# A transformer block with Hedgehog linear attention: the sums of exponentials read in another order, and two softmaxes of the first block moved

## The chip, the cores and the metric

The kernel runs on one core of a Trainium2 chip. The metric is device time in microseconds (us) of one execution, the median of several. The core has a matrix engine (TensorE, PE in the profile, its weight loads PEld), a vector engine (VectorE, DVE), an engine for pointwise functions (ScalarE, ACT), a programmable one (GpSimd, POOL) and SyncE (SP), which here issues nearly all DMAs. Matmuls write PSUM, which VectorE and ScalarE read; all else lies in SBUF, 128 partitions wide.

## The reference

There are S = 2048 tokens of width 576, 32 heads of width 18, and a hidden width of 4608. What it computes, cut to the core:

```python
mod = silu(c) @ w_mod                      # six rows: sa, ca, ga, sb, cb, gb
h   = layernorm(x) * (1 + ca) + sa
q, k, v = split(h @ wqkv)                  # 32 heads of 18
pq, pk  = q @ w_phi[h], k @ w_phi[h]       # per head, 18 -> 18
phi_q = concat(softmax(pq), softmax(-pq))  # 36 features a head
phi_k = concat(softmax(pk), softmax(-pk))
kv, z = phi_k^T v, sum over s of phi_k
o = (phi_q kv) / (phi_q z + 1e-6)
x = x + ga * (o @ wo)
h = layernorm(x) * (1 + cb) + sb
x = x + gb * (relu(h @ w1) @ w2)
```

Each softmax is over the 18 features of one head of one token, so every token needs 64 sums of 18 exponentials for its queries and as many for its keys.

## The kernel before, in words

**Tiles.** Tokens lie in 16 tiles of 128 partitions. Heads are packed three to a group, 11 groups (the last has two heads and a zero one). Within a group the 54 columns are ordered by feature slot f (18) and then by head h (3): column f*3 + h. Beside them lie the 54 columns of the negated half, so a group's exponentials are 108 columns, first half s = 0, second half s = 1. A key tile holds its 11 groups at a distance of 108 elements (`phik`), a query pair in `Eqs` at a distance of 128. Elements are bf16, two bytes.

**Softmax** (`softmax_parts`, lines 392 to 485). For a block of four key tiles or a pair of query tiles (U = 2): `low` and `high` find minimum and maximum of every head by a tree of VectorE instructions (L401 to L406) and subtract them into the two halves (L412, L415); each is also there in parts, `low_root`, `low_less(j)`, `high_root`, `high_less(j)`. `exps(j)` takes the exponentials of one tile on ScalarE (L443). Then come the sums over the 18 slots, in one of two ways. `sums_pe(j)` (L445 to L452) sums for two tiles on TensorE: 18 matmuls, one for each slot f, with the identity as weights, accumulate 132 columns (2 tiles x 11 groups x 2 halves x 3 heads) in PSUM. `sums(j)` (L454 to L459) sums one tile on VectorE in one reduction. `recip(j)` takes Ln and Exp with scale -1 on ScalarE (L465, L467), and `scale(j)` multiplies the exponentials on VectorE (L474 for keys, L479 for queries). `split` is true for keys, whose sums are stored tile by tile.

**Order.** Scheduling is by hand: every engine runs its instructions in the order in which the program issues them. Phase 1 (up to line 753) follows a written list of steps, `order`: the folded weights, the norm, the projections (L385, one helper for k, v, q and the output projection), the keys' softmax with its eight `sums_pe` (steps `SU`), the softmax of query pair 0 with one (`qSU`), `phi_k^T v` (L564), and the first attention output. Phase 2 runs `block(n)` for the eight pairs of tiles n = 0 to 7. Block n does the feed-forward of pair n: `ffn1` for three hidden groups at a time (nine groups q, matmuls at L789 and L782, Relu on ScalarE at L794 with further work issued behind it), and `ffn2_step` in thirds of 12 matmuls (L821, then two VectorE instructions at L825 and L826 and a store). Between these it does the attention of pair n + 1: `attention(j)` is `num` (L605), the quotient on VectorE (L615 to L619) and a transpose by DMA (L630); `late(j)` is the output projection, the residual (L654) and the statistics; `norm_out` normalises and transposes by DMA (L363); `mods` modulates (L356). And it does the softmax of pair n + 2, ending in `q_T(n + 2)`, two DMA transposes from SP (L592) into `ET`, which `num` of the next block loads as weights.

**Block 0** is an exception: it also has the softmax of pair 1 (`soft1`), which its own attention needs. Before the change both `soft1` and the third pair's `soft_` (pair 2) do `low` and `high` first; pair 1's sums go to TensorE behind the fifth Relu; pair 2's exponentials go behind the seventh and eighth Relu, its sums, reciprocal, scaling and transposes to the end of the block, around the modulation.

Of the kernel before, what the change touches and what calls it, by code (L numbers as in the profile page):

```python
# [12 lines left out]
ACT = mybir.ActivationFunctionType  # L13
# [7 lines left out]
U = 2  # L21
# [20 lines left out]
def kernel(  # L42
# [34 lines left out]
    def aux_tile(name, dt=FP32):  # L77
        t = aux.tile([P, 512], FP32, name=name, tag="aux")
        return t if dt == FP32 else t.bitcast(BF16)
# [312 lines left out]
    def softmax_parts(E, src, n, split):  # L392

        ng = n * NG

        def view(j, s):
            return E[:, j, :, s * GF:(s + 1) * GF].rearrange("p g (f h) -> p g f h", h=GH)

        def ext(op):
            a9 = work.tile([P, 4 * NG, 27], BF16, name="tree", tag="tree", bufs=1)[:, 0:ng]  # L400
            V.tensor_tensor(out=a9.rearrange("p (n g) c -> p n g c", g=NG), in0=src[:, :, :, 0:27],  # L401
                            in1=src[:, :, :, 27:54], op=op)
            for w in (12, 6, 3):
                V.tensor_tensor(out=a9[:, :, 0:w], in0=a9[:, :, 0:w], in1=a9[:, :, w:2 * w], op=op)  # L404
            r = work.tile([P, 4 * NG, GH], BF16, name="root", tag="root", bufs=4)[:, 0:ng]
            V.tensor_tensor(out=r, in0=a9[:, :, 0:3], in1=a9[:, :, 24:27], op=op)  # L406
            return r.rearrange("p (n g) h -> p n g h", g=NG)

        def less(j, mn, mx):
            f = src[:, j].rearrange("p g (f h) -> p g f h", h=GH)  # L410
            if mx is None:
                V.tensor_tensor(out=view(j, 1), in0=mn[:, j].unsqueeze(2).to_broadcast([P, NG, DH, GH]),  # L412
                                in1=f, op=ALU.subtract)
            else:
                V.tensor_tensor(out=view(j, 0), in0=f,  # L415
                                in1=mx[:, j].unsqueeze(2).to_broadcast([P, NG, DH, GH]), op=ALU.subtract)

        t = {}

        def low_root():  # L420
            t["mn"] = ext(ALU.min)

        def low_less(j):
            less(j, t["mn"], None)

        def high_root():
            t["mx"] = ext(ALU.max)

        def high_less(j):
            less(j, None, t["mx"])  # L430

        def low():
            low_root()
            for j in range(n):
                low_less(j)

        def high():
            high_root()
            for j in range(n):
                high_less(j)  # L440

        def exps(j):
            A_.activation(out=E[:, j], in_=E[:, j], func=ACT.Exp)  # L443

        def sums_pe(j):  # L445

            ps = aux_tile("ps_sum")
            t[j] = ps[:, 0:2 * 2 * NG * GH]
            e = (E[:, j:j + 2].rearrange("p n g (s c) -> p n (g s) c", s=2) if split else
                 E[:, j:j + 2].rearrange("p n g (s c) -> p (n g) s c", s=2))  # L450
            for f in range(DH):
                T_.matmul(t[j], lhsT=ident[:], rhs=e[:, :, :, f * GH:(f + 1) * GH], start=(f == 0), stop=(f == DH - 1))  # L452

        def sums(j):  # L454
            if j == 0:
                t["l"] = work.tile([P, 132], FP32, name="ln_s", tag="ln_s", bufs=2)
                t[0] = t["l"][:]
            V.tensor_reduce(out=t["l"][:, j * 66:(j + 1) * 66].rearrange("p (g s h) -> p g s h", s=2, h=GH), op=ALU.add,
                            axis=mybir.AxisListType.X, in_=E[:, j].rearrange("p g (s f h) -> p g s h f", s=2, h=GH))  # L459

        def recip(j):
            ln_s = t.get("l")
            if ln_s is None:
                ln_s = work.tile([P, 132], FP32, name="ln_s", tag="ln_s", bufs=2)
            A_.activation(out=ln_s[:], in_=t[j], func=ACT.Ln)  # L465
            t["r", j] = work.tile([P, 132], BF16, name="rsum", tag="rsum", bufs=3)
            A_.activation(out=t["r", j][:], in_=ln_s[:], func=ACT.Exp, scale=-1.0)  # L467

        def scale(j):
            r = t["r", j][:].rearrange("p (a s h) -> p a s h", s=2, h=GH)  # L470
            if split:
                for i in range(2):
                    e = E[:, j + i].rearrange("p g (s f h) -> p (g s) f h", s=2, h=GH)
                    V.tensor_tensor(out=e, in0=e, in1=t["r", j][:, i * 66:(i + 1) * 66].rearrange("p (a h) -> p a h", h=GH)  # L474
                                    .unsqueeze(2).to_broadcast([P, 22, DH, GH]), op=ALU.mult)
                return
            for s in range(2):
                e = E[:, j:j + 2, :, s * GF:(s + 1) * GF].rearrange("p n g (f h) -> p (n g) f h", h=GH)
                V.tensor_tensor(out=e, in0=e, in1=r[:, :, s, :].unsqueeze(2).to_broadcast([P, 2 * NG, DH, GH]), op=ALU.mult)  # L479

        class parts:
            pass
        for f in (low_root, low_less, high_root, high_less, low, high, exps, sums_pe, sums, recip, scale):
            setattr(parts, f.__name__, staticmethod(f))
        return parts
# [101 lines left out]
    def q_T(n):  # L587
        E = Es[n]
        ET = work.tile([P, NG, U, P], BF16, name="ET", tag="ET", bufs=2)
        ETs[n] = ET  # L590
        for j in range(U):
            nc.sync.dma_start_transpose(out=ET[:, :, j, :], in_=E[:, j].rearrange("p g c -> p (g c)"))  # L592
# [243 lines left out]
    def block(n):  # L836


        m = n + 1 if n + 1 < NQ else None
        if m is None:  # L840
            for qs in ((0, 1, 2), (3, 4, 5), (6, 7, 8)):
                ffn1(n, qs)
            y(n, 0)

            y(n, 1, ((0, 288), (288, 192), (480, 96)))
            return
        soft_ = q_soft(n + 2) if n + 2 < NQ else None
        xn, stats, rstd, norm = norm_stats(m * U, U)

        def do(name, *a):  # L850
            if soft_ is not None:
                getattr(soft_, name)(*a)

        def attention(j):
            num(m, j)
            o_T(m, j)

        def late(j):
            wo_res(m, j)
            stats(j)  # L860

        def norm_out():
            rstd()
            norm()
            norm_dma(xn, U, new_hT2(m), 0)

        def mods():
            for ci in range(KC):
                modulate(V, hT2[m][:, ci, :], hT2[m][:, ci, :], mod[2], ci)

        if n == 0:
            soft1 = q_soft(1)
            for x in (soft1, soft_):
                x.low()
                x.high()
            ffn1(n, (0, 1, 2), {1: lambda: soft1.exps(0), 2: lambda: soft1.exps(1)})
            ffn1(n, (3, 4, 5), {4: lambda: soft1.sums_pe(0)})
            soft1.recip(0)
            soft1.scale(0)
            q_T(1)  # L880
            ffn1(n, (6, 7, 8), {6: lambda: do("exps", 0), 7: lambda: do("exps", 1)})
            ffn2_step(n, 0, 0, 288, 0)
            attention(0)
            ffn2_step(n, 0, 0, 288, 1)
            attention(1)
            ffn2_step(n, 0, 0, 288, 2)
            ffn2_step(n, 0, 288, 288, 0)
            late(0)
            ffn2_step(n, 0, 288, 288, 1)
            late(1)  # L890
            norm_out()
            do("sums", 0)
            ffn2_step(n, 0, 288, 288, 2)
            do("sums", 1)
            mods()
            do("recip", 0)
            do("scale", 0)
            q_T(n + 2)
            y(n, 1)
            return  # L900
        do("low")
        do("high")
        ffn1(n, (0, 1, 2), {1: lambda: attention(0)})
        ffn1(n, (3, 4, 5), {(3, "pairs"): lambda: attention(1), 3: lambda: do("exps", 0), 4: lambda: do("exps", 1),
                            5: lambda: late(0)})
        do("sums", 0)
        ffn1(n, (6, 7, 8), {7: lambda: late(1)})
        norm_out()
        do("sums", 1)
        ffn2_step(n, 0, 0, 288, 0)  # L910
        ffn2_step(n, 0, 0, 288, 1)
        ffn2_step(n, 0, 0, 288, 2)
        do("recip", 0)
        do("scale", 0)
        if n + 2 < NQ:
            q_T(n + 2)
        ffn2_step(n, 0, 288, 288, 0)
        mods()
        ffn2_step(n, 0, 288, 288, 1)
        ffn2_step(n, 0, 288, 288, 2)  # L920
        y(n, 1)
# [31 lines left out]
```

## Time and profile before

| | before |
|---|---|
| median of 3 runs | 435.09 us (435.04 to 435.96) |
| the profiled execution's own time | 435.43 us |
| its span, first to last instruction | 433.7 us |
| TensorE busy | 425.7 us (98%), 4147 matmuls |
| VectorE, ScalarE busy | 248.5 us (57%), 177.5 us (41%) |
| sums on TensorE (L452) | 180 matmuls |
| sums on VectorE (L458) | 12 reductions |
| granted TensorE clock, mean | 0.992 |

The page of the profile has the busy time of each engine, the span in 40 slices with the granted TensorE clock in tenths, the chain of work that ended last (followed back from the end, at each step to what released it), and the costliest groups of instructions. Matmuls are pipelined: the duration of a single matmul's row is longer than the time by which it delays the next, so what a matmul costs is read from the distance of starts, or from a group's length in the chain divided by its count.

### The profile page before, as it was taken

Reading aid. Unit: us, or ns where it says so; the run is one execution under the profiler, and the core shown is the slowest. Engines: PE = TensorE matmul, PEld = TensorE weight load, DVE = VectorE, ACT = ScalarE, POOL = GpSimd, SP = SyncE. Lnnn points to the kernel's source line nnn. Section 1 sums busy time; section 2 is a strip of 40 time slices with the busy share of each in tenths; the row PEclk is TensorE's granted clock in tenths of the full one; section 3 lists DMA queues with packets and bytes.
Section 4 is the critical chain, followed back from the end, with each engine's and each line's share of the span. In section 5 each row is a group of like instructions: output and inputs, shape, how many; then the busy total and the mean of one; then the engine's idle time right before and its main releaser. Section 6 shows DMA issues by size and latency. Waiting matters only on the chain.

```text
span 433.7 us, 9654 instructions
## 1 busy us (share of the span) xinstructions
PE 425.7 (98%) x4147; PEld 349.7 (81%) x4147; DVE 248.5 (57%) x627; ACT 177.5 (41%) x293; POOL 16.8 (4%) x55
## 2 busy tenths in 40 slices
PE   8999999999999998999999999999999999999997
PEld 4877888888788777878888887888788888878886
DVE  5998999986673695556562746455464712421011
ACT  4875987775466015402620451063026104302510
POOL 8300000000000000000000000000000000000000
PEclk9889999999999999999999999999999999999999
DMA  8965322008996154050114106110502231010000
GB/s 267 377 193 91 32 21 42 2 5 151 400 388 177 33 70 89 0 112 15 32 30 82 30 17 77 49 32 17 98 15 30 47 81 32 2 44 15 2 2 27
DMA packets 67188, 34.93 MB, mean 81 GB/s; under 512 B 53833, under 2 KB 63946, under 8 KB 67018
## 3 DMA queue, kind: packets, MB, share of 16 engines
q1 hardware_dynamic: 66544, 34.30, 32.2%
q8 instruction: 32, 0.52, 0.5%
q10 hardware_dynamic: 602, 0.02, 0.1%
q14 instruction: 10, 0.08, 0.1%
HBM read 19.63 MB, written 2.36 MB: 51 GB/s over the span
## 4 chain that ended last, share of the span: by engine, by line
PE 90%; DMA 5%; DVE 3%; SPq 1%; ACT 1%; issue 0%; DVEq 0%
PE ps_y L821 30%; PE ps_h L789 29%; PE ps_q L385 5%; PE ps_sum L452 4%; PE ps_k L385 4%; PE ps_wo L385 4%; PE ps_h L782 4%; PE ps_v L385 4%; DMA wma<-in_w_mod_dram 2%; DMA ET<-room 1%; PE ps_kv L564 1%; DMA oT<-o_tm 1%; PE ps_num L605 1%; DVE bst L190 1%; PE ps_mod L275 1%; PE ps_row L342 1%
## 5 line engine op out<-in xcount | busy, mean ns | idle before, releaser
L794 ACT ACTIVATE H<-ps_h 128x1024 bf16<-128x1024 f32 x72 | 73.6, 1022 | 173.0 <-PE ps_h L782 124.5
L821 PE MATMUL ps_y<-w_sb,H 128*128 128x288 bf16 (+2 forms) x1188 | 143.2, 282 | 0.0
L821 PEld LDWEIGHTS <-H 128*128 128x128 bf16 x1188 | 113.7, 98 | 27.3
L789 PE MATMUL ps_h<-hT,w1a 128*128 128x256 bf16 x640 | 74.9, 273 | 0.0
L789 PEld LDWEIGHTS <-w1a 128*128 128x128 bf16 x640 | 60.9, 98 | 10.3 <-issue 3.4
L825 DVE TENSOR_TENSOR outt<-ps_y,row_gb 128x288 bf16<-128x288 f32 (+2 forms) x33 | 14.8, 447 | 83.3 <-PE ps_y L821 83.2
L789 PE MATMUL ps_h<-hT,w1b 128*128 128x256 bf16 x512 | 60.5, 273 | 0.0
L385 PEld LDWEIGHTS <-hT 128*128 128x128 bf16 x480 | 46.4, 98 | 12.6 <-issue 1.0
L789 PEld LDWEIGHTS <-w1b 128*128 128x128 bf16 x512 | 49.5, 98 | 7.6 <-issue 1.7
L654 DVE TENSOR_TENSOR x_sb<-x_sb,ps_wo 128x288 bf16<-128x288 bf16 x28 | 12.7, 454 | 40.8 <-PE ps_wo L385 40.8
L404 DVE TENSOR_TENSOR tree<-tree 128x132 bf16<-128x132 bf16 (+3 forms) x72 | 24.4, 339 | 2.5
L190 DVE BATCH_NORM_STATS2 bst<-x_sb 128x6 f32<-128x288 bf16 x64 | 25.7, 443 | 0.1
L385 PE MATMUL ps_v<-wv_sb,hT 128*128 128x288 bf16 x160 | 21.7, 286 | 0.9 <-DVE room L85 0.9
L385 PE MATMUL ps_wo<-wo_sb,oT 128*128 128x288 bf16 x160 | 22.1, 286 | 0.5 <-DMA oT<-o_tm 0.5
L385 PE MATMUL ps_k<-wfold,hT 128*128 128x270 bf16 (+1 forms) x160 | 22.3, 291 | 0.0
L385 PE MATMUL ps_q<-wfold,hT 128*128 128x270 bf16 (+1 forms) x160 | 20.9, 285 | 0.0
L199 DVE TENSOR_SCALAR xn<-x_sb,mv,rstd 128x576 bf16<-128x576 bf16 x32 | 13.0, 452 | 12.1 <-ACT rstd L195 12.0
L782 PE MATMUL ps_h<-hT,w1c 64*128 64x256 bf16 x288 | 19.9, 271 | 0.0
L452 PEld LDWEIGHTS <-ident 128*128 128x128 bf16 x180 | 18.2, 103 | 1.4
L443 ACT ACTIVATE phik<-phik 128x1188 bf16<-128x1188 bf16 x16 | 18.7, 1187 | 1.2 <-DVE phik L415 1.1
L443 ACT ACTIVATE room<-room 128x1188 bf16<-128x1188 bf16 x16 | 18.9, 1185 | 0.7 <-DVE room L415 0.7
L385 PEld LDWEIGHTS <-oT 128*128 128x128 bf16 x160 | 15.5, 98 | 4.4 <-DMA oT<-o_tm 0.8
(139 smaller groups left out, 378.4 us busy)
## 6 DMA issues: line engine op xcount, KB each, us to landing
w_sb<-in_B_w_dram SPq DMA_DIRECT2D x4, 1296.0 KB, 15.6
out_dram<-outt SPq DMA_DIRECT2D x15, 144.0 KB, 1.9
w1b<-in_B_w_dram SPq DMA_DIRECT2D x1, 2048.0 KB
w1a<-in_B_w_dram SPq DMA_DIRECT2D x1, 1536.0 KB, 11.3
wma<-in_w_mod_dram SPq DMA_DIRECT2D x1, 1152.0 KB, 7.8
room<-in_A_wqkv_dram SPq DMA_DIRECT2D x2, 576.0 KB, 8.5
x_sb<-in_A_x_dram SPq DMA_DIRECT2D x1, 1152.0 KB, 9.8
wmb<-in_w_mod_dram SPq DMA_DIRECT2D x1, 1152.0 KB, 12.7
```

Of the source, the lines that this page charges most:

```text
L190: V.bn_stats(out=st[:, half, :], in_=x_sb[:, t0 + j, half * 288:(half + 1) * 288])
L199: V.tensor_scalar(out=xn[:, j, 0:D], in0=x_sb[:, t0 + j, :], scalar1=mv[:, j, 0:1], scalar2=rs[:, j:j + 1], op0=ALU.subtract, op1=ALU.mult)
L385: T_.matmul(ps[:, 0:cn], lhsT=lhs[:, ci, :], rhs=w[:, ci, cs:cs + cn], start=(ci == 0), stop=(ci == KC - 1))
L404: V.tensor_tensor(out=a9[:, :, 0:w], in0=a9[:, :, 0:w], in1=a9[:, :, w:2 * w], op=op)
L443: A_.activation(out=E[:, j], in_=E[:, j], func=ACT.Exp)
L452: T_.matmul(t[j], lhsT=ident[:], rhs=e[:, :, :, f * GH:(f + 1) * GH], start=(f == 0), stop=(f == DH - 1))
L654: V.tensor_tensor(out=xs[:, cs:cs + cn], in0=xs[:, cs:cs + cn], in1=p[:, 0:cn], op=ALU.add)
L782: T_.matmul(ps[q][:, e, hh * w:hh * w + w], lhsT=w1c[r, 2 * q + hh, :], rhs=hT[r, 4, :], start=(first and hh == 0), stop=(not first and hh ...
L789: T_.matmul(ps[q][:, e, hh * w:hh * w + w], lhsT=w1_at(4 * q + 2 * hh + e, ci), rhs=hT[:, ci, :], start=(first and hh == 0 and ci == 0), s ...
L794: A_.activation(out=H1[:, 4 * q:4 * q + 4, :].rearrange("p (h e) n -> p e h n", e=2), in_=ps[q][:].rearrange("p e (h n) -> p e h n", h=2), ...
L821: T_.matmul(ps[:, 0, 0:cn], lhsT=H1[:, k, j * P:(j + 1) * P], rhs=w2_sb[:, k, c], start=(k == 0), stop=(k == NJ - 1))
L825: V.tensor_tensor(out=o[:, c], in0=ps[:, 0, 0:cn], in1=rows["gb"][:, c], op=ALU.mult)
```

## The change

Two things change. First, the order in which `sums_pe` reads the exponentials of one slot: before, group by group with the three heads of a group next to each other; after, the head is the outermost of the free dimensions and the groups and halves the innermost. The sums then lie in PSUM in that order, and `recip` reads them by a rearranged view, so that `ln_s` and all after it are as before. `sums` gives its view of `ln_s` the same form.

Second, in block 0: `soft1`'s sums move from TensorE to VectorE, two reductions ahead of the second `ffn1`, with its reciprocal behind the fifth Relu. `soft_` (pair 2) is spread over the block: its maximum tree before `soft1`'s scaling, its subtraction of the maximum behind `q_T(1)`, its sums and reciprocal before the first third of `ffn2`, and its scaling and `q_T(2)` behind the second `attention`, where before they stood at the end.

```diff
         def sums_pe(j):
 
-            ps = aux_tile("ps_sum")
-            t[j] = ps[:, 0:2 * 2 * NG * GH]
-            e = (E[:, j:j + 2].rearrange("p n g (s c) -> p n (g s) c", s=2) if split else
-                 E[:, j:j + 2].rearrange("p n g (s c) -> p (n g) s c", s=2))
+            ps = aux_tile("ps_sum")[:, 0:2 * 2 * NG * GH]
+            if split:
+                e = E[:, j:j + 2].rearrange("p n g (s f h) -> p f h n (g s)", s=2, h=GH)
+                t[j] = ps.rearrange("p (h a) -> p a h", h=GH)
+            else:
+                e = E[:, j:j + 2].rearrange("p n g (s f h) -> p f h s (n g)", s=2, h=GH)
+                t[j] = ps.rearrange("p (h s a) -> p a s h", h=GH, s=2)
             for f in range(DH):
-                T_.matmul(t[j], lhsT=ident[:], rhs=e[:, :, :, f * GH:(f + 1) * GH], start=(f == 0), stop=(f == DH - 1))
+                T_.matmul(ps, lhsT=ident[:], rhs=e[:, f], start=(f == 0), stop=(f == DH - 1))
...
-            A_.activation(out=ln_s[:], in_=t[j], func=ACT.Ln)
+            o = ln_s[:].rearrange("p (a h) -> p a h", h=GH) if split else ln_s[:].rearrange("p (a s h) -> p a s h", s=2, h=GH)
+            A_.activation(out=o, in_=t[j], func=ACT.Ln)
...
             soft1 = q_soft(1)
-            for x in (soft1, soft_):
-                x.low()
-                x.high()
+            soft1.low()
+            soft1.high()
+            soft_.low()
             ffn1(n, (0, 1, 2), {1: lambda: soft1.exps(0), 2: lambda: soft1.exps(1)})
-            ffn1(n, (3, 4, 5), {4: lambda: soft1.sums_pe(0)})
-            soft1.recip(0)
+            soft1.sums(0)
+            soft1.sums(1)
+            ffn1(n, (3, 4, 5), {4: lambda: soft1.recip(0)})
+            soft_.high_root()
             soft1.scale(0)
             q_T(1)
-            ffn1(n, (6, 7, 8), {6: lambda: do("exps", 0), 7: lambda: do("exps", 1)})
+            for j in range(U):
+                soft_.high_less(j)
+            ffn1(n, (6, 7, 8), {6: lambda: soft_.exps(0), 7: lambda: soft_.exps(1)})
+            soft_.sums(0)
+            soft_.sums(1)
+            soft_.recip(0)
             ffn2_step(n, 0, 0, 288, 0)
             attention(0)
             ffn2_step(n, 0, 0, 288, 1)
             attention(1)
+            soft_.scale(0)
+            q_T(n + 2)
             ffn2_step(n, 0, 0, 288, 2)
             ffn2_step(n, 0, 288, 288, 0)
             late(0)
             ffn2_step(n, 0, 288, 288, 1)
             late(1)
             norm_out()
-            do("sums", 0)
             ffn2_step(n, 0, 288, 288, 2)
-            do("sums", 1)
             mods()
-            do("recip", 0)
-            do("scale", 0)
-            q_T(n + 2)
             y(n, 1)
```

More of the change, by code (lines that the diff above doesn't have):

```diff
@@ L456, in sums @@
                 t["l"] = work.tile([P, 132], FP32, name="ln_s", tag="ln_s", bufs=2)
-                t[0] = t["l"][:]
+                t[0] = t["l"][:].rearrange("p (a s h) -> p a s h", s=2, h=GH)
             V.tensor_reduce(out=t["l"][:, j * 66:(j + 1) * 66].rearrange("p (g s h) -> p g s h", s=2, h=GH), op=ALU.add,
```

## The prediction

> **What bounds the kernel now.** I read the page first (busy time, granted clock, the chain), then the chain in order of time, then every view of line 452, where the sums of exponentials are made.
>
> ```profile
> PE 425.7 (98%) x4147; PEld 349.7 (81%) x4147; DVE 248.5 (57%) x627; ACT 177.5 (41%) x293; POOL 16.8 (4%) x55
> ...
> PEclk9889999999999999999999999999999999999999
> ...
> PE 90%; DMA 5%; DVE 3%; SPq 1%; ACT 1%; issue 0%; DVEq 0%
> ```
>
> TensorE bounds the kernel: 98% busy, and 90% of the chain. A nanosecond added to its queue is a nanosecond of kernel, unless it fills one of its few holes. The chain in order of time shows the sums among the projections (a start, a length, the group):
>
> ```profile
> 28.91 2.00 PE ps_k L385 x10
> ...
> 49.27 1.92 PE ps_sum L452 x18
> 51.19 1.23 PE ps_k L385 x10
> ...
> 65.37 3.86 PE ps_sum L452 x36
> ...
> 82.17 2.01 PE ps_sum L452 x18
> ...
> 115.15 0.45 PE psT_n L369 x8
> ...
> 127.63 2.01 PE ps_sum L452 x18
> ```
>
> From 44 to 117 us the chain is TensorE without a gap, and ten sums lie on it: eight of keys (18 matmuls in 1.92 us, 106.7 ns each), two of queries (2.01 us, 111.7 ns each). That is slow. A projection's ten matmuls of 288 columns on average take 1.23 us, 0.427 ns a column, so 132 columns should take 56 ns; eight transposes of 128 columns, each with its own weights, do take 0.45 us, 56 ns each. What differs is the moving operand: for one slot it reads 44 runs of three elements (6 bytes), 108 bytes apart. The view of line 452 says what such runs cost (duration min/median/max in ns):
>
> ```profile
> L452 PE MATMUL ps_sum<-phik,ident x144: 268/275/282, 49.1 to 97.0; 128*128 128x132 bf16 x144
> L452 PE MATMUL ps_sum<-room,ident x36: 237/279/326, 82.0 to 129.4; 128*128 128x132 bf16 x36
> ```
>
> Key matmuls are all alike, query matmuls spread over 89 ns, with the same 44 runs and the same weights. Stepping through the timeline of the group at 127.47, starts follow each other after 128, 95, 130, 149, 96, 128, 94, 77 ns, and then again 126, 96, 128, 144, 95, 130, 95, 76. The period is 8 slots, 48 bytes: it is the address that counts. Query groups lie 256 bytes apart and their halves 108, and a boundary every 16 bytes fits: in slots 0, 2, 3 and 5 half of the runs straddle one (66 pieces), in 1, 4, 6 and 7 none does (44 pieces). For keys all halves lie 108 bytes apart, so a quarter straddles in every slot: 55 pieces, always alike. The time goes by pieces: (95+96+94+77)/4 = 90 ns for 44 is 2.06 ns a piece, (128+130+149+128)/4 = 134 for 66 is 2.03, 106.7 for 55 is 1.94; the lowest slot gives 77/44 = 1.75, the highest 149/66 = 2.26.
>
> **The change, part by part.**
>
> *The order of reading.* The new operand runs over the 44 groups and halves inside and the three heads outside. Neighbouring reads are now 108 or 256 bytes apart: 132 pieces of one element, not 55 of two or three. No row shows one-element pieces alone. Bounds: 1.75 x 132 = 231 ns a matmul and 2.26 x 132 = 298; below these stands only the contiguous 56 ns (a rival). I take 245 ns, 1.85 a piece: under the keys' 1.94, since a piece of one element has least to hand over, and above the one best slot. Keys: 144 x (245 - 106.7) = +19.9 us. The query sum that stays on TensorE (pair 0): 18 x (245 - 111.7) = +2.4. Together +22.3, all on the chain; with the bounds +20.0 to +30.9. VectorE and ScalarE get slack by it, so nothing is late behind them. [...]
>
> *The Ln.* Its nine inputs (L465, 0.28 us each) are now read from PSUM in steps and written in the old order. Bounds: nothing, or twice as long, 2.5 us on ScalarE in all; a gain is not excluded but would be as idle. Each stands between a sum and a scaling with other TensorE work between; I take 0.
>
> *First block: pair 1's sums on VectorE.* TensorE loses the group at 127.63: -2.0 us. VectorE gains two reductions:
>
> ```profile
> L458 DVE TENSOR_REDUCE ln_s<-room x12: 1334/1382/1384, 151.6 to 340.3; 128x66 f32<-128x1188 bf16 x12
> ```
>
> The timeline has the room for them on VectorE, and the wait that the next part is about on TensorE (start, length, idle before in brackets):
>
> ```profile
> 133.00 1.88 DVE L479 TENSOR_TENSOR room<-room,rsum 128x1188 bf16<-128x1188 bf16 x2 [4.68 <-ACT rsum L467]
> ```
>
> ```profile
> 164.50 0.41 PE L605 MATMUL ps_num<-KVZ,ET 108*128 108x57 bf16 x8 [1.18 <-DMA ET<-room]
> ```
>
> Two by 1.3 us fill most of the 4.68 us that VectorE idles ahead of its scaling. On times of before: they start when the third pair's subtraction from the minimum ends (125.5; the exponentials are done at 125.7) and end at 128.2; Ln and Exp behind the fifth Relu (ends 128.7) are done at 129.3, so the sixth Relu, queued behind them, starts about when its matmuls end; the maximum tree ends at 129.9, scaling at 131.8. The two transposes are issued 3.1 us earlier, and TensorE needs them 2.0 earlier: not late. Without VectorE's hole these reductions would cost up to 2.6 us.
>
> *First block: pair 2's softmax moved.* Nothing is added: the two subtractions, two exponentials, two reductions, Ln, Exp, two scalings and two transposes are done earlier. The exponentials wait for subtractions that end at 132.3 and 132.8, as Relus 7 and 8 (131.5 and 133.7) finish, so Relu 8 behind the first is not held. The reductions fall into VectorE's 4.36 us of idling ahead of the first quotient (139.24 in before, 137.2 now), the second until 137.4: +0.2 us for that quotient and for the transposed outputs behind it, where TensorE already waits 0.49 us at 147.27. I count +0.2 (bounds 0 and +1). The scaling, 1.88 us, now stands ahead of an output's eviction and the first residual; VectorE idled 1.28 us there and again 1.32 before the second, so it is covered. On SP the two transposes pass the output store and the transposes of the normalised rows (issued from 151.76) and stand behind those of the attention output; SP has nothing between 144 and 151.7, and their issue takes 3.98. POOL's fills of o_tm are not passed. What goes is the wait of the row at 164.50: TensorE waits 1.18 us there for ET, issued at 159.01. Next in line is the modulated hT, done at 157.15 against TensorE's need at 158.9: 1.7 us of margin, so the whole -1.2 is had.
>
> **Sum.** 435.43 (the profiled execution: span 433.7 and 1.7 around it) + 22.3 - 2.0 - 1.2 + 0.2 = 454.7; it ran 0.3 above the median of 435.09, so 454.4 us. Bounds 231 and 298 give 452.1 and 463.0.
>
> **Rivals.**
>
> *The clock drops in the sums* (chance 0.30). Each stretch, us, then busy time of TensorE, weight loads, VectorE, ScalarE, POOL, and the granted clock:
>
> ```profile
> 26.00:29.41 3.41, 3.41 (x80) 3.00 (x78) 3.31 (x13) 2.38 (x8) 0.28 (x1) 1.00 0.78 224
> 29.42:32.83 3.41, 3.41 (x19) 2.15 (x17) 3.31 (x12) 2.86 (x8) 0.00 (x0) 0.50 0.09 20
> ```
>
> The first stretch was full of matmuls by count, but 60 of them have one column; streamed columns fill about a third of it. In the next 3.41 us the clock is 0.50, and ten ps_k at 28.91 take 2.00 us, not 1.23. The sums now stream 56/245 = 23% (before 53%, where the clock held), and a group of 18 lasts 4.4 us, longer than such a stretch. If waiting for operands counts as idle, most of the seven places with sums (five single, two double) bring a drop that costs the work behind it up to 1.7 us; at 1.0 each, +7: 461 us, between 458 and 470. Against: nobody has idled; the array is held, not empty. [...]
>
> *Not slower: the price hangs on the weights, not on the order* (0.07). Each sum matmul loads the identity anew (180 loads, 103 ns mean), near the 106.7 ns spacing; if the load sets it, the order changes nothing and only block 0 moves: 435.1 - 3.0 = 432.1. This decides if a one-element piece costs under 0.8 ns. Against: 56 ns transposes also load 128 columns each time, and the query slots' 77 to 149 ns. [...]
>
> *Faster: the price is per run* (0.06). Six runs of 22 would stand in place of 44 of three; at the contiguous 56 ns, 144 x 50.7 + 18 x 55.7 = 8.3 us less: 423.8. For it: short runs are slow now. Against: with runs unchanged, straddling alone moves the price from 95 to 130.
>
> **How the numbers follow.** The forecast has 0.57; with the clock's rival 0.87 for slower. Faster has the other two, 0.12, less 0.01 for the weights' rival with block 0's gain lost. About 0.2% is what a measurement here can tell from no change. The range runs from the low bound less what the pieces' price may still be under (448) to the clock's rival with most of its spread (468): of the 0.87 it leaves out some 0.05, so it holds 0.82.
>
> **What the profile will show.** Right: groups of ps_sum x18 of about 4.4 us in the chain, 162 and not 180 matmuls on that line, none after 117 us plus the shift; two more reductions on VectorE (14); no wait for ET at the first num of block 1; from there to the end the blocks unchanged. Clock rival: stretches at 0.5 behind the sums. Wrong: a group of 1.0 us (price per run) or still 1.9 (weights).

## The result, and the profile after

The changed kernel takes 464.11 us (460.28 to 466.24), before it took 435.09: 6.5% slower, ratio 1.0652 with a 95% interval of 1.0578 to 1.0726. That lies inside the range that was given (448 to 468), 9.7 us above the forecast of 454.4 and 3 above the first rival's 461: the forecast's price came true, and the rival's drops of the clock came on top of it. The profiled execution took 465.03 us, its span is 463.2. The spread of the changed kernel, 6 us, is new; before it was 0.9.

The same lines of the page of after: busy time, granted clock in 40 slices, the chain by engine and by line.

```profile
PE 455.5 (98%) x4129; PEld 356.3 (77%) x4129; DVE 252.6 (55%) x629; ACT 177.6 (38%) x293; POOL 16.8 (4%) x55
...
PEclk9799879797889999999999999999999999999999
...
PE 90%; DVE 5%; DMA 3%; ACT 1%; issue 0%; SPq 0%
PE ps_y L825 29%; PE ps_h L793 27%; PE ps_sum L455 9%; PE ps_q L385 5%; PE ps_wo L385 4%; PE ps_v L385 4%; PE ps_k L385 4%; PE ps_h L786 4%; DVE bst L190 2%; DMA wma<-in_w_mod_dram 2%; PE ps_kv L568 1%; DMA oT<-o_tm 1%; PE ps_num L609 1%; DVE xn L199 1%; DVE mv L191 1%; DVE room L85 0%
```

TensorE has 18 matmuls less and is busy 30 us longer, and the clock, full after the start before, now has dents in slices 5 to 12 (0.86 as the mean from 40 to 150 us). The chain in order of time has both (start, length, group):

```profile
49.20 1.23 PE ps_bias L329 x10
50.43 4.58 PE ps_sum L455 x18
55.01 2.40 PE ps_k L385 x10
57.41 2.40 PE ps_v L385 x10
...
75.51 9.13 PE ps_sum L455 x36
84.64 5.12 PE ps_k L385 x30
...
101.69 4.09 PE ps_sum L455 x18
105.77 2.35 PE ps_v L385 x10
```

A key group takes 4.58 us (254 ns a matmul; 106.7 before), the query group 4.09 (227 ns). And projections right behind take 2.40 us for ten, not 1.23. The account up to the first matmul of the first feed-forward (117.0 us before, 149.9 after, +32.9) closes:

| | us |
|---|---|
| the nine sums of phase 1: 4.58 + 4.55 + 9.13 + 4.57 + 4.09 + 4.57 + 9.13 = 40.6, before 17.4 | +23.2 |
| slowed groups behind them: three of ten by 1.17, ps_q 0.17, ps_k 1.44, ps_v 1.12, ps_q 1.08, ps_kv 1.14 | +8.5 |
| the start, up to ps_bias (49.20, before 48.04) | +1.2 |
| block 0 and the wait in block 1: 313.3 us from the first feed-forward matmul to the end, before 316.65 | -3.3 |

The sum is +29.6 us, the difference of the spans (463.2 - 433.7 = 29.5). The start isn't the change's: up to 49 us the two programs differ in nothing that runs, and the first experiment's profile, with the old order, has the same lateness (first feed-forward matmul at 118.5).

That the slowed groups are the clock's work is in the view by stretches of after, which are cut on the grid of 3.41 us on which the clock changed in this trace (length, TensorE busy and count, weight loads, VectorE, ScalarE, POOL, then the granted clock):

```profile
49.92:53.33 3.41, 3.41 (x18) 1.75 (x16) 3.17 (x8) 2.54 (x5) 0.90 (x2) 1.00 0.96 43
53.33:56.74 3.41, 3.41 (x16) 1.98 (x15) 3.20 (x8) 0.59 (x2) 0.00 (x0) 0.50 0.00 0
...
94.29:97.70 3.41, 3.41 (x21) 2.06 (x20) 1.95 (x5) 2.18 (x4) 0.00 (x0) 1.00 0.02 5
...
101.12:104.53 3.41, 3.41 (x19) 1.86 (x18) 1.34 (x4) 2.17 (x2) 0.00 (x0) 1.00 0.00 0
104.53:107.94 3.41, 3.41 (x16) 2.03 (x15) 0.00 (x0) 1.13 (x3) 0.00 (x0) 0.50 0.00 0
```

TensorE counts as busy without a gap in all of them. Adding up streamed columns at 0.427 ns each (a projection's 1.23 us for 2880; an estimate), the stretch from 49.92 has 30% and the one from 101.12 has 34%, and each is followed by one at half clock; the one from 94.29 has 55% and the one from 97.70 has 41%, and the clock held behind both.

### The profile page after: what moved, and what is told of

Same layout as the page of the kernel before. It is cut to its first block, busy times and chain, and to the rows that moved or that the text cites. A ratio compares the mean times of both kernels' runs of the same rounds, so it can differ in the third digit from the quotient of the medians.

```text
span 463.2 us, 9618 instructions
## 1 busy us (share of the span) xinstructions
PE 455.5 (98%) x4129; PEld 356.3 (77%) x4129; DVE 252.6 (55%) x629; ACT 177.6 (38%) x293; POOL 16.8 (4%) x55
## 3 DMA queue, kind: packets, MB, share of 16 engines
HBM read 19.63 MB, written 2.36 MB: 47 GB/s over the span
## 4 chain that ended last, share of the span: by engine, by line
PE 90%; DVE 5%; DMA 3%; ACT 1%; issue 0%; SPq 0%
PE ps_y L825 29%; PE ps_h L793 27%; PE ps_sum L455 9%; PE ps_q L385 5%; PE ps_wo L385 4%; PE ps_v L385 4%; PE ps_k L385 4%; PE ps_h L786 4%; DVE bst L190 2%; DMA wma<-in_w_mod_dram 2%; PE ps_kv L568 1%; DMA oT<-o_tm 1%; PE ps_num L609 1%; DVE xn L199 1%; DVE mv L191 1%; DVE room L85 0%
## 5 line engine op out<-in xcount | busy, mean ns | idle before, releaser
L793 PEld LDWEIGHTS <-w1a 128*128 128x128 bf16 x640 | 60.9, 98 | 10.3 <-issue 3.4
L385 PEld LDWEIGHTS <-hT 128*128 128x128 bf16 x480 | 49.7, 105 | 17.6 <-issue 1.0
L455 PE MATMUL ps_sum<-phik,ident 128*128 128x132 bf16 x144 | 37.5, 436 | 0.0
L455 PEld LDWEIGHTS <-ident 128*128 128x128 bf16 x162 | 19.6, 121 | 19.7
L478 DVE TENSOR_TENSOR phik<-phik,rsum 128x1188 bf16<-128x1188 bf16 x16 | 15.0, 979 | 25.7 <-ACT rsum L471 25.7
L190 DVE BATCH_NORM_STATS2 bst<-x_sb 128x6 f32<-128x288 bf16 x64 | 25.7, 444 | 0.1
L385 PE MATMUL ps_k<-wfold,hT 128*128 128x270 bf16 (+1 forms) x160 | 25.4, 318 | 0.3 <-ACT room L83 0.3
L385 PE MATMUL ps_v<-wv_sb,hT 128*128 128x288 bf16 x160 | 24.1, 306 | 0.7 <-DVE room L85 0.4
L385 PE MATMUL ps_q<-wfold,hT 128*128 128x270 bf16 (+1 forms) x160 | 22.2, 297 | 0.0
L461 DVE TENSOR_REDUCE ln_s<-room 128x66 f32<-128x1188 bf16 x14 | 19.0, 1366 | 1.9 <-ACT room L443 1.9
```

The lines of the kernel that those rows point to most:

```text
L190: V.bn_stats(out=st[:, half, :], in_=x_sb[:, t0 + j, half * 288:(half + 1) * 288])
L385: T_.matmul(ps[:, 0:cn], lhsT=lhs[:, ci, :], rhs=w[:, ci, cs:cs + cn], start=(ci == 0), stop=(ci == KC - 1))
L455: T_.matmul(ps, lhsT=ident[:], rhs=e[:, f], start=(f == 0), stop=(f == DH - 1))
L793: T_.matmul(ps[q][:, e, hh * w:hh * w + w], lhsT=w1_at(4 * q + 2 * hh + e, ci), rhs=hT[:, ci, :], start=(first and hh == 0 and ci == 0), s ...
```

## The experiments

**The old order back.** The changed kernel, with `sums_pe` and `recip` as before:

```diff
-                e = E[:, j:j + 2].rearrange("p n g (s f h) -> p f h n (g s)", s=2, h=GH)
...
+            e = (E[:, j:j + 2].rearrange("p n g (s c) -> p n (g s) c", s=2) if split else
...
-                T_.matmul(ps, lhsT=ident[:], rhs=e[:, f], start=(f == 0), stop=(f == DH - 1))
+                T_.matmul(t[j], lhsT=ident[:], rhs=e[:, :, :, f * GH:(f + 1) * GH], start=(f == 0), stop=(f == DH - 1))
```

> The changed kernel with the old order of reading in sums_pe and recip; block 0 stays as changed. Theory (each separate piece of 16 bytes that a sum matmul touches costs about 1.9 ns, and the slow sums then let the clock drop): key groups are back at 1.92 us and query groups at 2.01, no stretch at clock 0.5 after 40 us, and block 0's two moves are all that is left: 435.1 - 2.0 - 1.2 + 0.2 = 432.1 us. Rival (block 0's moves cost something that the slow phase 1 hides, on VectorE or in the transposes): 435 or more, with a new wait in block 0.

Measured: 432.53 us beside 435.87 for the kernel before on the same chip, ratio 0.9926 (0.9913 to 0.9939). It was expected at 432.1. So the whole loss hangs on the order of reading, and block 0's moves are a gain of 3.3 us. This kernel is faster than both.

**The new order alone.** The reverse: the kernel before with the new `sums_pe` and `recip`, block 0 untouched.

> The kernel before with the new order of reading alone; block 0 as before, so ten groups of sums on TensorE. Theory: groups as in the changed kernel (4.57 us of keys, 4.09 of queries), the drops of the clock in phase 1, and one more slow group in block 0, 2.1 us longer: 464.1 + 4.1 + 1.2 - 0.2 = 469.2 us, some 34 above before, with a spread of several us between executions. Rival (the order costs only its matmul time, 8 x 2.65 + 2 x 2.08 = 25.4 us, and the rest of the 29 us came from block 0): 460.5.

Measured: 468.09 us (466.86 to 470.71), ratio 1.0752 (1.072 to 1.0783), 32.2 us above before; 469.2 was expected by the theory and 460.5 by the rival that took the matmul time alone. Its profile has half-clock stretches from 75.7 to 82.5, 96.2 to 113.2, 120.0 to 130.3 and 161.0 to 164.4 us, other places than in the changed kernel, though the groups are the same. Its grid of 3.41 us lies otherwise: one stretch starts at 51.78 us, in the changed kernel one at 49.92.

**Eighteen patterns in one kernel.** In the kernel before, the eighteen matmuls of each key sum read 132 elements in eighteen different patterns, one per line:

```diff
-            for f in range(DH):
-                T_.matmul(t[j], lhsT=ident[:], rhs=e[:, :, :, f * GH:(f + 1) * GH], start=(f == 0), stop=(f == DH - 1))
+            mm(o, lhsT=ident[:], rhs=x[:, 0:132], start=True, stop=False)
+            mm(o, lhsT=ident[:], rhs=st(2), start=False, stop=False)
...
+            mm(o, lhsT=ident[:], rhs=run(3, 24, 0), start=False, stop=False)
+            mm(o, lhsT=ident[:], rhs=run(3, 24, 6), start=False, stop=False)
...
+            mm(o, lhsT=ident[:], rhs=e[:, :, :, 17 * GH:18 * GH], start=False, stop=True)
```

Here `st(k)` reads every k-th element, and `run(m, k, o)` runs of m elements at a distance of k, from offset o (elements of two bytes).

> The kernel before, but the eighteen matmuls of each key sum read 132 elements in eighteen patterns, one on a line each: contiguous; single elements 4, 6, 8, 12, 16 and 18 bytes apart; 44 runs of three 48 bytes apart, starting on a 16-byte boundary or straddling one; 66 runs of two 32 bytes apart, likewise; 33 runs of four 64 bytes apart, likewise; 22 runs of six 96 apart; runs of four 16 apart; single elements 36 bytes apart; the new order; the old order. The sums of the keys are therefore not the reference's: the true sums are left out. Theory of pieces (about 1.9 ns for each 16-byte piece, or 0.42 a column where that is more): contiguous 56 ns; 4 bytes apart 33 pieces, 63 ns; 8 apart 66 pieces, 127; 16 and more apart 132 pieces, 253; runs of three aligned 44 pieces, 84, and straddling 88 pieces, 169; runs of two 127 and 253; runs of four 63 and 127; runs of four 16 bytes apart 63. Rival (a price per jump, each step that is not to the next element): all patterns of single elements alike at about 253, runs of three 84 whether they straddle or not, runs of two 127, runs of four 63. Rival (the weights' load): all near 107.

The chain of this kernel, one matmul a row (start, length):

```profile
49.17 0.06 PE ps_sum L466
49.23 0.06 PE ps_sum L467
49.29 0.09 PE ps_sum L468
49.38 0.12 PE ps_sum L469
49.49 0.18 PE ps_sum L470
49.67 0.23 PE ps_sum L471
49.90 0.24 PE ps_sum L472
50.15 0.08 PE ps_sum L473
50.23 0.16 PE ps_sum L474
50.38 0.12 PE ps_sum L475
50.50 0.24 PE ps_sum L476
50.74 0.06 PE ps_sum L477
50.80 0.11 PE ps_sum L478
50.91 0.06 PE ps_sum L479
50.97 0.06 PE ps_sum L480
51.03 0.23 PE ps_sum L481
51.27 0.26 PE ps_sum L482
51.53 0.11 PE ps_sum L483
```

| line | pattern | 16-byte pieces | us | ns a piece |
|---|---|---|---|---|
| L466 | contiguous | 17 | 0.06 | columns set it |
| L467 | single elements 4 bytes apart | 33 | 0.06 | 1.8, or the columns |
| L469 | single, 8 apart | 66 | 0.12 | 1.8 |
| L470 | single, 12 apart | 99 | 0.18 | 1.8 |
| L471 | single, 16 apart | 132 | 0.23 | 1.7 |
| L473 | runs of three, aligned | 44 | 0.08 | 1.8 |
| L474 | runs of three, straddling | 88 | 0.16 | 1.8 |
| L475 | runs of two, aligned | 66 | 0.12 | 1.8 |
| L476 | runs of two, straddling | 132 | 0.24 | 1.8 |
| L477 | runs of four, aligned | 33 | 0.06 | 1.8, or the columns |
| L478 | runs of four, straddling | 66 | 0.11 | 1.7 |
| L482 | the new order | 132 | 0.26 | 2.0 |
| L483 | the old order | 55 | 0.11 | 2.0 |

The time goes with the pieces, at 1.7 to 2.0 ns each, as long as the columns don't take longer; the five patterns that the table leaves out fit as well. Why the two orders of the kernel pay 2.0 and the other patterns 1.7 to 1.8 isn't shown. That the pieces are of 16 bytes is in the single elements: 0.06, 0.12, 0.18 and 0.23 us at 4, 8, 12 and 16 bytes, and no more than 0.24 at 18 (L472). A price per jump is out: single elements cost 0.06 to 0.24 us with 132 jumps each, and 66 runs of two double their time by a shift of 14 bytes (L475, L476). The weights are out: all eighteen load the same identity and take 0.06 to 0.26 us. The patterns also say what the new order did: 132 elements out of 132 pieces, where the old order got them out of 55.

**Dense matmuls in between.** To tell whether the low share of streaming brings the drops, the changed kernel gets a matmul of 324 columns between each two matmuls of a sum (contiguous for keys, three runs of 108 for the query sum):

```diff
-            ps = aux_tile("ps_sum")[:, 0:2 * 2 * NG * GH]
+            full = aux_tile("ps_sum")
+            ps = full[:, 0:2 * 2 * NG * GH]
...
             for f in range(DH):
+                if f:
+                    T_.matmul(full[:, 132:456].rearrange("p (g c) -> p g c", g=3), lhsT=ident[:], rhs=E[:, j, 0:3], start=False, stop=False)
                 T_.matmul(ps, lhsT=ident[:], rhs=e[:, f], start=(f == 0), stop=(f == DH - 1))
```

> The changed kernel with a matmul of 324 contiguous columns between each two of a sum's matmuls, into columns of the same bank that nobody reads: 17 more in each of nine groups, 153 by 0.138 us = 21.1 us more work on TensorE, which raises the share of time in which columns stream within a group from 22% to about 48%. Theory (the drops come from sums that stream too little within a window of 3.41 us; in the changed kernel windows under 0.35 dropped and those from 0.40 did not): no stretch at clock 0.5 between 40 us and the end, which gives the 8.5 us of slowed projections back: 464.1 + 21.1 - 8.5 = 476.7 us, and a spread between executions of under 1 us as before the change. Rival (the drops come with time, or the slowed projections have another cause): 485 us, with the same stretches at 0.5.

Measured: 478.07 us (475.9 to 478.9). Of the chain, a sum's matmul and the projections right behind the first sum:

```profile
50.33 0.26 PE ps_sum L458
...
57.21 1.23 PE ps_k L385 x10
```

The view by stretches of this kernel, one in the middle of a double group and one over all of phase 1:

```profile
83.07:86.48 3.41, 3.41 (x19) 1.88 (x18) 1.63 (x4) 0.00 (x0) 0.00 (x0) 1.00 0.01 2
...
40.00:160.00 120.00, 120.00 (x949) 81.69 (x947) 66.99 (x137) 53.98 (x112) 1.21 (x4) 1.00 0.21 46
```

The clock is 1.00 throughout; in the changed kernel it is 0.86 between 40 and 150 us. The sums still take 0.25 us each, and the projections behind them are back at 1.23 us for ten. The time is 1.4 us from the theory's 476.7 and 7 from the rival's 485: 21.1 us of added work cost 14.0. That the share of streaming brings the drops is shown; the spread stayed at 3 us, against the theory's 1, and that is open.

**Block 0, one move at a time**, both with the old order of reading, as edits of the kernel before. First only pair 1's:

```diff
-            for x in (soft1, soft_):
-                x.low()
-                x.high()
+            soft1.low()
+            soft1.high()
+            soft_.low()
...
-            ffn1(n, (3, 4, 5), {4: lambda: soft1.sums_pe(0)})
-            soft1.recip(0)
+            soft1.sums(0)
+            soft1.sums(1)
+            ffn1(n, (3, 4, 5), {4: lambda: soft1.recip(0)})
+            soft_.high_root()
...
+            for j in range(U):
+                soft_.high_less(j)
```

> The old order of reading, and of block 0's changes only pair 1's (its sums on VectorE, and what was put around them); pair 2's sums, reciprocal, scaling and transposes stand at the end of the block as before. Theory: TensorE has one group of 2.0 us less and nothing else moves on the chain; the wait for ET at the first num of block 1 stays at about 1.2 us: 435.4 - 2.0 = 433.4 us, 0.9 above the kernel with both. Rival (VectorE's two reductions come late for the first transposes): 434.5 or more, with a wait for ET in block 0.

Then only pair 2's, with pair 1's sums on TensorE as before:

```diff
+            do("sums", 0)
+            do("sums", 1)
+            do("recip", 0)
             ffn2_step(n, 0, 0, 288, 0)
             attention(0)
             ffn2_step(n, 0, 0, 288, 1)
             attention(1)
+            do("scale", 0)
+            q_T(n + 2)
...
-            do("sums", 0)
             ffn2_step(n, 0, 288, 288, 2)
-            do("sums", 1)
             mods()
-            do("recip", 0)
-            do("scale", 0)
-            q_T(n + 2)
```

> The old order of reading, pair 1 as before the change (its sums on TensorE), and only pair 2's sums, reciprocal, scaling and transposes moved ahead, as in the change. Theory: the wait for ET at the first num of block 1 is gone, 1.2 us, less 0.2 for the first quotient: 435.4 - 1.0 = 434.4 us. Rival (the transposes moved ahead get in the way of the attention output's, so that the output projection waits longer): 435.4 or more, with a longer wait for oT than 0.5 us.

Measured, beside 435.47 for the kernel before: 432.81 (ratio 0.994, 0.992 to 0.9959) and 433.56 (0.9955, 0.9939 to 0.9972). Two rows of the timelines show the first num of block 1, first in the kernel with pair 1 alone:

```profile
161.86 0.41 PE L605 MATMUL ps_num<-KVZ,ET 108*128 108x57 bf16 x8 [0.74 <-DMA ET<-room]
```

and then in the one with pair 2 alone:

```profile
162.72 0.40 PE L605 MATMUL ps_num<-KVZ,ET 108*128 108x57 bf16 x8
```

Pair 2's move takes the wait for ET away, as said. Pair 1's alone leaves it, but at 0.74 us, not 1.18. From the first feed-forward matmul to the end, before takes 316.65 us, pair 1 alone 313.54, pair 2 alone 314.93, both 313.34: gains of 3.1, 1.7 and 3.3. They don't add up, since a wait for oT at the output projections comes and goes: before has 0.49 us at the second (147.27), pair 2 alone 0.13 there, pair 1 alone none, and both together 0.53 at the first:

```profile
144.06 1.40 PE L385 MATMUL ps_wo<-wo_sb,oT 128*128 128x288 bf16 x10 [0.53 <-DMA oT<-o_tm]
```

That is the kernel with the old order and both moves. Its two transposes land 3.7 us after their issue, as in the changed kernel; before, with either move alone and in the two kernels below they land after 2.6. In the experiment with two slots below, block 0 is the same code and has no such wait (from its first matmul to block 1's first it takes 39.12 us there, 39.83 here), so it isn't the moved transposes alone that bring it. What makes them land later was not found.

**Longer runs.** If pieces are the price, a sum should read several slots at a time. With the old order and block 0 as changed, three slots at once, or two; VectorE adds the parts in one reduction out of PSUM:

```diff
-            for f in range(DH):
-                T_.matmul(t[j], lhsT=ident[:], rhs=e[:, :, :, f * GH:(f + 1) * GH], start=(f == 0), stop=(f == DH - 1))
+            for f in range(0, DH, 3):
+                T_.matmul(t[j], lhsT=ident[:], rhs=e[:, :, :, f * GH:(f + 3) * GH], start=(f == 0), stop=(f == DH - 3))
...
+                V.tensor_reduce(out=ln_s[:].rearrange("p (a h) -> p a h", h=GH), op=ALU.add, axis=mybir.AxisListType.X,
+                                in_=t[j].rearrange("p (a q h) -> p a h q", q=3, h=GH))
```

> Block 0 as changed; sums_pe reads three neighbouring slots at once, so 6 matmuls of 396 columns in runs of nine elements (18 bytes), and VectorE adds the three sums (one reduction out of PSUM, some 0.5 us, for each of nine groups). Theory of pieces: 88 pieces by 1.8 ns are 158 ns, under the 168 ns that 396 columns take, so a group lasts 1.0 us in place of 1.92 or 2.0: 9 x 0.9 = 8 us less on TensorE; VectorE gets 4.5 us more in phase 1, where it is about 90% busy, so that 0 to 4.5 of it come back as waits: 424.5 to 429 us against 432.5 with block 0 alone. Rival (VectorE becomes what phase 1 waits for): 432.5 or more.

> The same with two neighbouring slots at once: 9 matmuls of 264 columns in runs of six elements (12 bytes), the reduction on VectorE about 0.35 us. Theory of pieces: of 44 runs five in eight straddle a 16-byte boundary on average, 71.5 pieces by 1.8 ns are 129 ns, over the 113 ns of 264 columns, so a group lasts 1.16 us: 9 x 0.77 = 6.9 us less, with 3 us more on VectorE: 425.5 to 428.5 us. Rival (VectorE becomes what phase 1 waits for): 432.5 or more.

Measured: 439.53 us (ratio 1.0087, 1.0064 to 1.0111) and 439.02 (1.008, 1.0056 to 1.0103), 7 and 6.5 above the kernel that has block 0's moves alone. Up to 429 and 428.5 were expected; the rival, 432.5 or more because phase 1 waits for VectorE, came true in both. The sums did get shorter: starts lie 212 ns apart with three slots (168 expected) and 132 with two (129 expected), so a group is 1.27 or 1.19 us, not 1.92. But the chain by engine and line of the kernel with three slots says where that went:

```profile
PE 73%; DVE 19%; ACT 4%; DMA 2%; issue 1%; SPq 0%; DVEq 0%
PE ps_y L827 31%; PE ps_h L795 29%; PE ps_wo L385 4%; PE ps_h L788 4%; DVE phik L480 3%; DVE tree L404 3%; PE ps_q L385 3%; DVE bst L190 2%; DVE phik L412 2%; DVE tree L401 2%; DMA oT<-o_tm 1%; DVE phik L415 1%; DVE xn L199 1%; DMA wk_raw<-in_A_wqkv_dram 1%; DVE ln_s L468 1%
```

and its view by stretches over phase 1:

```profile
44.00:118.00 74.00, 63.85 (x617) 46.69 (x615) 63.91 (x129) 48.58 (x97) 1.21 (x4) 0.98 0.28 53
```

VectorE has 19% of the chain (3% before), and TensorE stands idle for 10 of 74 us that it filled before. The nine reductions take 0.56 us each, 5.1 together, and hang between a sum and the scaling that waits for it. Behind idle time the clock drops as well, in both kernels: with three slots it is 0.98 in this view, and ten projections at 108.63 us take 2.36 us in place of 1.23; with two slots ten at 109.17 take 2.24. In phase 1 VectorE (busy 63.9 of these 74 us) is near enough to its limit that time added to it comes out as time. Whether shorter sums without added work on VectorE would gain was not run.

## Why the prediction held, and where it was off

The time lies in the range because the range took in the clock's rival. The forecast's own sum was 454.7 for the profiled execution, which took 465.03, and its highest price gave 463.0 at the median, under the 464.11 measured. The 10.3 us that are missing are 8.5 of the clock, 0.9 of the price and 1.2 of a late start that isn't the change's, less 0.3 that block 0 gained more.

- *The price of the new order.* Right, by its mechanism and nearly by its size: 245 ns a matmul were taken, 254 measured for keys and 227 for queries, +23.2 us for +22.3. The key's 1.92 ns a piece stands right by the 1.94 of the old order. That a piece with one element should cost less than one with more, for which 1.85 was taken, is borne out only by the queries (227/132 = 1.72); in the eighteen patterns single elements and runs of three pay the same, 1.7 to 1.8. Of the ten sums that the prediction counts between 44 and 117 us, nine lie there and the tenth at 127.63, but its sum takes that one out with block 0, so nothing hangs on it.
- *All of it on the chain.* Right: sums, slowed groups and the late start account for the shift of the first feed-forward matmul without a remainder, and VectorE's new idle time behind them (25.7 us of waiting for ScalarE's reciprocals at the key scaling, from 1.8) cost nothing.
- *The clock.* This is where the forecast was off, by the rival that stood at 0.30. The step that failed is to leave it out of the sum because the array "is held, not empty". The clock fell to 0.50 behind stretches in which TensorE counts as busy for all of their 3.41 us (30% streaming from 49.92, 34% from 101.12): the work behind six of the seven places with sums was slowed by 1.1 to 2.3 us each, +8.5 us in the profiled execution, where the rival had +7 from 1.0 at all seven. Dense matmuls between those of a sum took the drops away, while the sums took as long as before. The rival's reading of the drop behind 26.00 was the right one, and with 23% streaming against the 35% of a stretch that had dropped, the rival should have been the forecast.
- *The Ln.* Nothing was taken, and nothing it is: the rearranged read takes 280 ns as its median, as before.
- *Pair 1's sums.* Two microseconds were taken from TensorE's queue, as said; the reductions filled VectorE's hole, and ET for pair 1 wasn't late. With pair 1 alone the gain is 3.1 us rather than 2.0, since the wait for oT (0.49 us) and part of that for ET (1.18 to 0.74) went as well.
- *Pair 2's softmax.* The wait of 1.18 us is gone, and the margin of hT held. The +0.2 for later attention outputs had the wrong reason: the quotient starts at once (138.69, num ends at 138.65), and the wait for oT that stayed, now at the first output projection, comes from transposes that land after 3.7 us and not 2.6.
- *The rivals on the other side.* Weights and price per run both fell with the eighteen patterns.
- *Block 0 in sum:* -3.3 where -3.0 was said.

## What to carry to other kernels

For a matmul with few columns, count how many separate 16-byte pieces of a partition its moving operand touches, not how many runs or jumps it has: here each cost 1.7 to 2.0 ns, as much as four columns, so that single elements 16 or more bytes apart took four times the contiguous time, 8 bytes apart twice, and 4 bytes apart no more than contiguous ones. Here the clock fell to 0.50 behind stretches of 3.41 us in which TensorE counted as busy throughout but streamed 22 to 39% of the columns of gapless projections, and ten ordinary matmuls behind such a stretch took 2.40 us, not 1.23: look at streamed columns too, not at busy time alone. Dense matmuls in between kept the clock up (1.00 from 40 to 160 us), but only work that has to be done anyway pays; the added ones here made the kernel 14 us slower. Before making such a read faster, see which engine stands next in line; here VectorE was busy 62 of the 73 us from 44 to 117, and a sum that got 0.7 us shorter on TensorE and 0.6 longer on VectorE lost.

## What the runs showed of the hardware beyond that

- A half-clock stretch didn't always last 3.41 us. The changed kernel has three of 6.83 us after 40 us (from 53.33, 80.64 and 125.01), and the kernel with the new order alone one of 17.07 (from 96.15). Counted in columns, in the traces of before and after, cut into stretches of 3.413 us on the grid of their clock, from 24 us to shortly before the end: all ten stretches that streamed at most about 3110 columns were followed by half clock, three of them at half clock themselves. All 234 with at least about 3270 were followed by full clock, seven of them at half clock themselves. Gapless projections would stream about 8000 in 3.413 us (2880 in 1.23; an estimate), so the two counts are 39 and 41% of that. What lies between was not met in these two traces.
- The clock's changes lie on a grid of 3.413 us in each of these two traces, to within 0.01 us, and its place against the program differed: the changed kernel and the one with the new order alone run the same program up to 49 us, and a stretch starts at 49.92 in one and at 51.78 in the other. With sums that stream 22% the time spreads over 6 us, with those of before over about 2 (434.5 to 436.8 in the largest set); that the place of the grid makes this spread is the author's estimate.
- Runs of nine elements (18 bytes, always two pieces) took 212 ns for 396 columns, 0.54 ns a column, above both the 168 of the columns and the 158 of 88 pieces at 1.8. Neither count alone gives that time; what adds to it isn't shown.
